# Attention, two networks: k times v with its mixed block last, and the weight work of the last two tiles of the first network held back

## The chip, the cores and the metric

One core of a Trainium2 chip. The time is that of the device for one execution, in microseconds (us). The kernel before has a median of 899.63 us over 3 runs (899.12 to 900.37).

## The reference

```python
def phi(x):                       # x: 4 batches, 8 heads, 576 positions, 64 dims; omega: 128 x 64
    proj = np.einsum('bhsd,md->bhsm', x, omega)
    sq = np.sum(x * x, axis=-1, keepdims=True) / 2.0
    h = proj - sq
    h = h - np.max(h, axis=-1, keepdims=True)
    return np.exp(h) / np.sqrt(m)
q_p, k_p = (phi(q_s), phi(k_s))
kv = np.einsum('bhsm,bhsd->bhmd', k_p, v)
z = np.sum(k_p, axis=2)
num = np.einsum('bhsm,bhmd->bhsd', q_p, kv)
den = np.einsum('bhsm,bhm->bhs', q_p, z)[..., None] + 1e-06
x = num / den                     # then as 2304 tokens of 512
h = x @ w_in                      # 512 x 2048
y = (h * (1.0 / (1.0 + np.exp(-1.702 * h)))) @ w_out
out = ((y @ w_a) * (y @ w_b)) @ w_out2     # 512 x 1536, twice, and 1536 x 512
```

q, k, v, omega and the output are float32, the weights float64. The kernel works in float16 pairs: every number is a high part and a low part (the rest), and a product is three matmuls, high by high, high by low and low by high.

## The kernel before

**Stages.** The attention of batch b gives one tile of 512 tokens (4 blocks of 128 positions a head); the 64 positions left over in each batch are collected to a fifth tile of 256, the rest tile. While the first network works on tile b - 1, the attention of batch b and the preparation of weights run beside it as generators, one step of each a turn (`side_step`, `run`). The last two tiles of the first network, tile 3 (512 tokens) and the rest tile, have no attention beside them. Then the second network runs over all tiles.

**k times v (lines 508 to 534, batches 2 and 3).** For each pair of heads there are nine blocks of k features (`e16`, high and low): four of the first head, four of the second, and a mixed block, index 2 * NT = 8, which holds the left-over rows of both heads and writes 130 columns where the others write 65. All nine sum up in one PSUM bank `pk`. The pool of such banks (`att`) has two, which the projections of all head pairs and `pk` share; a projection's bank comes free when ScalarE has read it (the exponentials, line 446). The mixed block is the last to be converted (lines 456, 457).

**One unit of the first network (lines 648 to 687).** `h_unit(f)` makes 128 hidden features: 12 matmuls into `ph`, tanh on ScalarE (line 662), `th` on VectorE (665), the high part `gh` on ScalarE (671), the low part `gl` on VectorE (672). `y_unit(f)` multiplies gh and gl by w_out, 12 matmuls. The order on TensorE is y(f), h(f+2), y(f+1), h(f+3), and so on; `ph` has two banks. `main` yields after each of them, 32 times in a 512 tile, 30 times in the rest tile.

**Weight work (`w_ops`, lines 203 to 278).** The weights come as 64-bit numbers and are made into float16 pairs in chunks of 1 MB. A chunk is: a load on SP's queue; on VectorE three integer operations of 1024 elements (lines 214, 254, 262); for the second network four sums of 256 elements into a scratch tile `sx` (line 248); high parts on ScalarE (272); low parts on VectorE (221: 512, 256 and 1024 elements). It is cut into five steps, in this order: line 214 of this chunk and 254; low parts of the chunk before; 262; the sums and high parts; 214 of the next chunk. The chunks 20 to 25 (NWE to NW2: 31 steps) belong to the last two tiles. `run` asks for `rate` steps for each yield of the tile; inside `tc.issue_after(ins)` each instruction on the engine of `ins` is queued behind `ins`, instructions of other engines are not.

```python
    def run(gen, rate, wmax):
        due = 0.0
        for _ in gen:
            due += rate
            if rate < 1:
                with tc.issue_after(own["nb"]):
                    w_steps(int(due), wmax)
```

`own["nb"]` is the last bias of an attention phase (line 486). In tile 3 no attention is left, so it is long past.

**The forms (`y_forms`, lines 731 to 767).** For the second network (seven products in place of eight) sums of quarters of y are made, split in high and low parts on ScalarE (745) and VectorE (741). Their scratch tile `ts` has the tag `sx` as the weight sums have, with one buffer. `y_forms(0)` is written in the rest tile, one step a yield; `y_forms(1)` in the second network, whose tiles `sums` open when the first network's memory closes.

**What sets the order.** The kernel is written in one order; the framework then makes each engine's queue from it as a list: of what is ready on an engine, the earliest written goes first, and a later one goes when nothing earlier is ready. The queue is fixed when the program is built, and an engine takes it in order.

Of the kernel before, what the change touches and what calls it, by code (L numbers as in the profile page):

```python
# [33 lines left out]
def fused_kernel(  # L34
# [13 lines left out]
    nc = tc.nc  # L48
    B, H, S, D = q.shape
# [4 lines left out]
    NT = 4  # L54
# [6 lines left out]
    T = 2 * NT + 1  # L61
# [125 lines left out]
    NW2 = len(chunks)  # L187
# [97 lines left out]
    def w_steps(n, upto):  # L285
        for _ in range(n):
            if w_done[0] < upto:
                w_done[0] = next(w_gen)
# [13 lines left out]
    own = {}  # L302
# [34 lines left out]
    def a_load(pool, kind, b, hp, queue=nc.sync):  # L337

        if b >= B or (kind, b, hp) in raws:
            return  # L340
        src = {"q": q, "k": k}[kind]
        h0 = 2 * hp
        place = kind
        if b == 0 and hp == NHP - 1:
            place = {"q": "k", "k": "q"}[kind]
        t = pool.tile([P, T, D], F32, tag=f"raw{place}", name=f"raw{kind}_{b}_{hp}", bufs=RAW[place])
        queue.dma_start(
            out=t[:, 0 : 2 * NT, :].rearrange("p (h t) d -> p h (t d)", h=2),
            in_=src[b, h0 : h0 + 2, 0:SM, :].rearrange("h (p t) d -> p h (t d)", t=NT),
        )  # L350
        queue.dma_start(out=t[:, 2 * NT, :], in_=src[b, h0 : h0 + 2, SM:S, :])
        raws[kind, b, hp] = t
# [149 lines left out]
    def kv_parts(hp, pk, scale):  # L502
        nc.scalar.activation(out=kvh[:, hp], in_=pk, func=AF.Copy, scale=scale)
        nc.vector.scalar_tensor_tensor(
            out=kvl[:, hp], in0=pk, scalar=scale, in1=kvh[:, hp], op0=ALU.mult, op1=ALU.subtract
        )

    def kphase32(pool, b, hp, psp, nxt, f32=True):
        nm = f"k{b}_{hp}"
        a_load(pool, "k", b, hp)  # L510
        raw = raws["k", b, hp]
        vt, vm = own["vt"][:, 2 * hp : 2 * hp + 2], own["vm"][:, hp]
        if not f32:
            e16 = pool.tile([P, 2, T, P], F16, tag="e16", name=f"e16_{nm}")
            yield from features(pool, nm, raw, e16, None, psp, nxt)
            v16 = pool.tile([P, 2, 2, NT + 1, VC], F16, tag="xf", name=f"v16_{nm}")
            for o, i in (v16[:, :, :, 0:NT], vt), (v16[:, :, :, NT], vm):
                nc.scalar.activation(out=o[:, 0], in_=i, func=AF.Copy, scale=S_V)
                nc.vector.scalar_tensor_tensor(
                    out=o[:, 1], in0=i, scalar=S_V, in1=o[:, 0], op0=ALU.mult, op1=ALU.subtract  # L520
                )
            yield
            pk = psp()[:, 0 : 2 * VC].rearrange("p (h c) -> p h c", h=2)
            for t in (2 * NT, *range(2 * NT)):
                hs, u = (slice(0, 2), NT) if t == 2 * NT else (t // NT, t % NT)
                eh, el = e16[:, 0, t], e16[:, 1, t]
                vh, vl = v16[:, 0, hs, u], v16[:, 1, hs, u]
                nc.tensor.matmul(pk[:, hs], eh, vh, start=(t == 2 * NT), stop=False)
                nc.tensor.matmul(pk[:, hs], eh, vl, start=False, stop=False)
                nc.tensor.matmul(pk[:, hs], el, vh, start=False, stop=(t == 2 * NT - 1))  # L530
            yield
            kv_parts(hp, pk, S_KV / (S_E * S_V))
            yield
            return
        e32 = pool.tile([P, T, M], F32, tag="e16", name=f"e32_{nm}")
        yield from features(pool, nm, raw, None, e32, psp, nxt)
        pk = psp()[:, 0 : 2 * VC].rearrange("p (h c) -> p h c", h=2)
        nc.tensor.matmul(pk, e32[:, 2 * NT, :], vm, start=True, stop=False)
        for t in range(2 * NT):
            nc.tensor.matmul(  # L540
                pk[:, t // NT], e32[:, t, :], vt[:, t // NT, t % NT, :], start=False, stop=(t == 2 * NT - 1)
            )
        yield
        nc.scalar.copy(own["kv"][:, hp], pk)
        yield
# [98 lines left out]
    def ffn1(j, xh, xl, n):  # L644

        gh, gl, yacc, phs = {}, {}, {}, {}
# [11 lines left out]
        def h_unit(f, cs=range(KC)):  # L658
            h_products(f, cs)
            ph = phs.pop(f)  # L660
            th = mp.tile([P, 512], F32, tag="f32", name=f"th{j}_{f}")
            nc.scalar.activation(  # L662
                out=th[:, :n], in_=ph[:, :n], func=AF.Tanh, scale=0.5 * 1.702 / (S_X * S_W)
            )
            nc.vector.scalar_tensor_tensor(  # L665
                out=th[:, :n], in0=th[:, :n], scalar=1.0, in1=ph[:, :n], op0=ALU.add, op1=ALU.mult
            )
            GS = 0.5 * S_G / (S_X * S_W)
            a = gp.tile([P, 512], F16, tag="gh", name=f"gh{j}_{f}")
            b = gp.tile([P, 512], F16, tag="gl", name=f"gl{j}_{f}")  # L670
            nc.scalar.activation(out=a[:, :n], in_=th[:, :n], func=AF.Copy, scale=GS)  # L671
            nc.vector.scalar_tensor_tensor(  # L672
                out=b[:, :n], in0=th[:, :n], scalar=GS, in1=a[:, :n],
                op0=ALU.mult, op1=ALU.subtract,
            )
            gh[f], gl[f] = a, b

        def y_unit(f):
# [48 lines left out]
    def y_load(j, n):  # L727
        yfs[j] = late["pool"].tile([P, KC, 512], F32, tag="yf", name=f"yf{j}", bufs=1)
        nc.sync.dma_start(out=yfs[j][:, :, :n], in_=ys[j][:, :, :n])
# [299 lines left out]
    def side_step():  # L1029

        while waiting and waiting[0][0] <= turn[0]:
            live.append(waiting.pop(0)[1])
        for g in list(live):
            if next(g, live) is live:
                live.remove(g)
        turn[0] += 1
# [15 lines left out]
        waiting.append((turn[0] + t, counted(b, gen)))  # L1052
        waiting.sort(key=lambda w: w[0])

    def run(gen, rate, wmax):

        due = 0.0
        for _ in gen:
            due += rate
            if rate < 1:  # L1060
                with tc.issue_after(own["nb"]):
                    w_steps(int(due), wmax)
            else:
                w_steps(int(due), wmax)
            due -= int(due)
            side_step()

    def finish_side(b):
        while left[b]:
            side_step()  # L1070
# [58 lines left out]
    following = []  # L1129
# [14 lines left out]
    def next_tile(b, make):  # L1144
        def made():
            finish_side(b)
            following.append(make())
            return following[-1]

        return made  # L1150
# [49 lines left out]
                    run(head(following[-1], 3), 11 / 32, NW1 + 2)  # L1200
                run(following[-1][0](ahead, 3 if b == 2 else 2), 11 / 32, (NW1 + 2, NWE)[b - 2])
    late["pool"] = ctx.enter_context(tc.tile_pool(name="late", bufs=1))
    run(following[-1][0](next_tile(B - 1, rest_tile)), 18 / 32, NW2)
    y_load(0, SM)
    fg = y_forms(0, SM)
    for i, _ in enumerate(following[-1][0]()):
        next(fg, None)
        if i % 2:
            w_steps(1, NW2)
    for _ in fg:  # L1210
        pass
    w_need(NW2)
# [39 lines left out]
```

## Time and profile before

| | |
|---|---|
| median of 3 runs | 899.63 us (899.12 to 900.37) |
| the profiled execution | 899.4 us, its span 897.6 us |
| TensorE matmul (PE) busy | 872.3 us, 97% |
| VectorE (DVE) busy | 690.9 us, 77% |
| ScalarE (ACT) busy | 455.3 us, 51% |
| tile 3 on TensorE | some 386 to 468 us |
| the rest tile on TensorE | some 468 to 513 us |

Times in the rows are from the span's start. PE is TensorE, DVE VectorE, ACT ScalarE, SP the queue that issues most transfers. The time of a matmul in its row is longer than the distance to the next one's start, since they are pipelined; the same holds in small for VectorE.

### The profile page before, as it was taken

The page shows a single profiled execution, that of the slowest core. Times are in us where ns is not written, and L with a number is a line of the kernel's source. Part 1 is how long each engine was busy: PE and PEld are TensorE (multiplying, and loading weights), DVE is VectorE, ACT ScalarE, POOL GpSimd, SP SyncE. Part 2 cuts the span into 40 slices and gives each one's busy share as a digit, 9 for nine tenths or more (in the row PEclk, how much of TensorE's full clock was granted, in tenths as well). Part 3 has the DMA queues.
Part 4 walks back from the last instruction along what each step waited for, and adds up shares of the span by engine and source line. Part 5 has one row for each costly group of instructions (what it writes and reads, how often), then busy time and mean ns, then how long its engine had stood idle before and what let it go on. Part 6 is the DMA issues. An engine that isn't in the chain of part 4 may idle for free.

```text
span 897.6 us, 17390 instructions
## 1 busy us (share of the span) xinstructions
PE 872.3 (97%) x7094; PEld 626.3 (70%) x7094; DVE 690.9 (77%) x1244; ACT 455.3 (51%) x1087; POOL 1.4 (0%) x10
## 2 busy tenths in 40 slices
PE   8999999999999999999999999999999999999997
PEld 6864555644554455444448888888888888888886
DVE  5889999778797787999923399777999558566766
ACT  7777774677566776454323354544443122233221
POOL 0000000000000000000000000000000000000000
PEclk9999999999999999999999999999999999999999
DMA  7856895453674323885401055212332022223312
GB/s 205 242 142 162 205 228 197 120 120 82 137 161 110 75 40 67 146 259 222 135 7 49 24 177 175 106 43 83 134 126 83 5 40 84 83 99 125 87 39 71
DMA packets 129343, 105.35 MB, mean 117 GB/s; under 512 B 97776, under 2 KB 111088, under 8 KB 127216
## 3 DMA queue, kind: packets, MB, share of 16 engines
q1 hardware_dynamic: 128558, 103.66, 41.2%
q8 instruction: 55, 0.90, 0.4%
q10 hardware_dynamic: 706, 0.59, 0.2%
q14 instruction: 24, 0.20, 0.1%
HBM read 71.07 MB, written 17.69 MB: 99 GB/s over the span
## 4 chain that ended last, share of the span: by engine, by line
PE 59%; DVE 21%; DMA 7%; ACT 7%; issue 2%; ACTq 0%; SPq 0%; DVEq 0%
PE ph L655 3%; PE ph L654 3%; PE ph L656 3%; PE y L685 3%; PE y L686 3%; PE y L687 3%; DMA xt_k<-x_k 3%; PE oA L904 2%; PE oA L902 2%; PE oA L903 2%; PE pbA L811 2%; PE pbA L809 2%; PE pbA L810 2%; PE paA L809 2%; PE pa L568 2%
## 5 line engine op out<-in xcount | busy, mean ns | idle before, releaser
L686 PE MATMUL y<-gl,w_out 128*128 128x512 f16 (+1 forms) x320 | 114.4, 358 | 0.9 <-DVE gl L672 0.8
L687 PE MATMUL y<-gh,w_out 128*128 128x512 f16 (+1 forms) x320 | 114.2, 358 | 0.0
L685 PE MATMUL y<-gh,w_out 128*128 128x512 f16 (+1 forms) x320 | 111.9, 358 | 0.8 <-ACT gh L671 0.7
L654 PE MATMUL ph<-xT,w_in 128*128 128x512 f16 x256 | 97.1, 379 | 1.5 <-DMA xT<-x_q_3x 0.7
L655 PE MATMUL ph<-xT,w_in 128*128 128x512 f16 x256 | 97.1, 379 | 0.3 <-DVE xT L623 0.3
L656 PE MATMUL ph<-xT,w_in 128*128 128x512 f16 x256 | 97.1, 379 | 0.0
L665 DVE SCALAR_TENSOR_TENSOR th<-th,ph 128x512 f32<-128x512 f32 (+1 forms) x80 | 50.3, 629 | 39.9 <-ACT th L662 39.7
L662 ACT ACTIVATE th<-ph 128x512 f32<-128x512 f32 (+1 forms) x80 | 44.2, 553 | 48.8 <-PE ph L656 48.8
L671 ACT ACTIVATE gh<-th 128x512 f16<-128x512 f32 (+1 forms) x80 | 47.1, 588 | 42.0 <-DVE th L665 41.9
L672 DVE SCALAR_TENSOR_TENSOR gl<-th,gh 128x512 f16<-128x512 f32 (+1 forms) x80 | 50.7, 634 | 15.9 <-ACT gh L671 15.5
L809 PE MATMUL paA<-forms,w_a 128*128 128x256 f16 (+1 forms) x240 | 61.0, 262 | 1.6 <-DVE ca L828 0.8
L809 PE MATMUL pbA<-forms,w_b 128*128 128x256 f16 (+1 forms) x240 | 61.1, 262 | 0.9 <-DVE cb L828 0.9
L811 PE MATMUL pbA<-forms,w_b 128*128 128x256 f16 (+1 forms) x240 | 61.0, 262 | 0.0
L811 PE MATMUL paA<-forms,w_a 128*128 128x256 f16 (+1 forms) x240 | 61.0, 262 | 0.0
L810 PE MATMUL pbA<-forms,w_b 128*128 128x256 f16 (+1 forms) x240 | 61.0, 262 | 0.0
L810 PE MATMUL paA<-forms,w_a 128*128 128x256 f16 (+1 forms) x240 | 61.0, 262 | 0.0
L902 PE MATMUL oA<-w_o,ab 128*128 128x256 f16 x216 | 58.9, 273 | 1.6 <-ACT ab L860 0.9
L904 PE MATMUL oA<-w_o,ab 128*128 128x256 f16 x216 | 58.9, 273 | 0.6 <-DVE ab L861 0.5
L903 PE MATMUL oA<-w_o,ab 128*128 128x256 f16 x216 | 58.9, 273 | 0.0
L817 ACT COPY ka<-paA 128x512 f32<-128x512 f32 (+1 forms) x30 | 16.3, 543 | 78.2 <-PE paA L811 78.1
L910 DVE SCALAR_TENSOR_TENSOR o<-oA,o 128x512 f32<-128x512 f32 (+1 forms) x45 | 28.5, 633 | 34.2 <-PE oA L904 34.2
L687 PEld LDWEIGHTS <-w_out 128*128 128x128 f16 x320 | 31.4, 98 | 29.9 <-issue 3.0
(209 smaller groups left out, 2353.5 us busy)
## 6 DMA issues: line engine op xcount, KB each, us to landing
wraw<-in_moe_w_out_dram SPq DMA_DIRECT2D x14, 1024.0 KB
forms<-fd SPq DMA_DIRECT2D x8, 1792.0 KB
wraw<-in_moe_w_in_dram SPq DMA_DIRECT2D x8, 1024.0 KB
fd<-forms SPq DMA_DIRECT2D x4, 1792.0 KB
wraw<-in_moe_w_a_dram SPq DMA_DIRECT2D x6, 1024.0 KB
wraw<-in_moe_w_b_dram SPq DMA_DIRECT2D x6, 1024.0 KB
vt<-in_v_dram SPq DMA_DIRECT2D x16, 256.0 KB
rawq<-in_q_dram SPq DMA_DIRECT2D x16, 256.0 KB
```

The source lines that it names most:

```text
L654: nc.tensor.matmul(ph[:, :n], w[:, 0, c, fs], xh(c), start=(c == 0), stop=False)
L655: nc.tensor.matmul(ph[:, :n], w[:, 0, c, fs], xl(c), start=False, stop=False)
L656: nc.tensor.matmul(ph[:, :n], w[:, 1, c, fs], xh(c), start=False, stop=(c == KC - 1))
L685: nc.tensor.matmul(o, w[:, 0, f % 4, cs], gh[f][:, :n], start=(f == 0), stop=False)
L686: nc.tensor.matmul(o, w[:, 0, f % 4, cs], gl[f][:, :n], start=False, stop=False)
L687: nc.tensor.matmul(o, w[:, 1, f % 4, cs], gh[f][:, :n], start=False, stop=(f == FC1 - 1))
L809: nc.tensor.matmul(o[:, i], wh, xh, start=first, stop=False, skip_group_check=True)
L810: nc.tensor.matmul(o[:, i], wh, xl, start=False, stop=False, skip_group_check=True)
L811: nc.tensor.matmul(o[:, i], wl, xh, start=False, stop=final, skip_group_check=True)
L902: nc.tensor.matmul(bank[:, t], lh, wh, start=first, stop=False, skip_group_check=True)
L903: nc.tensor.matmul(bank[:, t], lh, wl, start=False, stop=False, skip_group_check=True)
L904: nc.tensor.matmul(bank[:, t], ll, wh, start=False, stop=final, skip_group_check=True)
```

## The change

The mixed block goes last in k times v. The weight steps of tile 3 are queued behind `gl` of the newest unit in place of `nb`, at 14 in 32 yields in place of 18; those of the rest tile are queued behind `gl` too, where nothing held them, at two in three yields in place of one in two.

```diff
-            for t in (2 * NT, *range(2 * NT)):
+            for t in range(T):
                 hs, u = (slice(0, 2), NT) if t == 2 * NT else (t // NT, t % NT)
                 eh, el = e16[:, 0, t], e16[:, 1, t]
                 vh, vl = v16[:, 0, hs, u], v16[:, 1, hs, u]
-                nc.tensor.matmul(pk[:, hs], eh, vh, start=(t == 2 * NT), stop=False)
-                nc.tensor.matmul(pk[:, hs], eh, vl, start=False, stop=False)
-                nc.tensor.matmul(pk[:, hs], el, vh, start=False, stop=(t == 2 * NT - 1))
+                nc.tensor.matmul(pk[:, hs], eh, vh, start=(t == 0), stop=False, skip_group_check=True)
+                nc.tensor.matmul(pk[:, hs], eh, vl, start=False, stop=False, skip_group_check=True)
+                nc.tensor.matmul(pk[:, hs], el, vh, start=False, stop=(t == T - 1), skip_group_check=True)
...
-            nc.vector.scalar_tensor_tensor(
+            own["gl"] = nc.vector.scalar_tensor_tensor(
                 out=b[:, :n], in0=th[:, :n], scalar=GS, in1=a[:, :n],
                 op0=ALU.mult, op1=ALU.subtract,
-            )
+            ).ins
...
-    def run(gen, rate, wmax):
+    def run(gen, rate, wmax, behind="nb"):
...
-                with tc.issue_after(own["nb"]):
+                with tc.issue_after(own[behind]):
                     w_steps(int(due), wmax)
...
-    run(following[-1][0](next_tile(B - 1, rest_tile)), 18 / 32, NW2)
+    run(following[-1][0](next_tile(B - 1, rest_tile)), 14 / 32, NW2, "gl")
     y_load(0, SM)
     fg = y_forms(0, SM)
     for i, _ in enumerate(following[-1][0]()):
         next(fg, None)
-        if i % 2:
-            w_steps(1, NW2)
+        if i % 3:
+            with tc.issue_after(own["gl"]):
+                w_steps(1, NW2)
```

## Rows read from the trace of the kernel before

**Rows 1.** Busy time by stage: tile 3, rest tile, start of the second network; clock, DMA.

```profile
core 0: us, PE busy (x) PEld busy (x) DVE busy (x) ACT busy (x) POOL busy (x), PEclk, DMA share, GB/s
...
386.00:468.00 82.00, 81.17 (x373) 36.38 (x372) 64.43 (x100) 35.53 (x59) 0.00 (x0) 1.00 0.46 154
468.00:513.00 45.00, 44.94 (x398) 38.72 (x397) 14.25 (x33) 15.14 (x38) 0.00 (x0) 1.00 0.07 25
513.00:560.00 47.00, 46.39 (x425) 41.25 (x423) 45.06 (x64) 24.64 (x42) 0.00 (x0) 1.00 0.52 177
```

**Rows 2.** Waits of TensorE: us in total, times, longest.

```profile
PE y L686 <- DVE gl L672: 0.8, 2, 0.4
...
PE ph L654 <- DMA xT<-x_q_3x: 0.7, 1, 0.7
```

**Rows 3.** What line 528, first matmul of a block, waited for (us, times).

```profile
  DVE sx L248: 0.8, 1
  ACT e_q L446: 0.6, 3
  ACT e_k L446: 0.4, 1
```

**Rows 4.** Timeline of TensorE: start, length, operation, [idle before].

```profile
205.15 0.22 PE L528 MATMUL pa<-v_k,e_k 128*128 128x130 f16 x1 [0.79 <-DVE sx L248]
```

**Rows 5.** Timeline of VectorE ahead of it: low half of the mixed block.

```profile
203.10 0.28 DVE L457 SCALAR_TENSOR_TENSOR e_k<-e_k,e_k 128x128 f16<-128x128 f32 x1
```

**Rows 6.** Timeline of ScalarE ahead of it: exponentials of another head pair.

```profile
203.97 1.12 ACT L446 ACTIVATE e_k<-pa,nb_k 128x128 f32<-128x128 f32 x4
```

**Rows 7.** Timeline of VectorE, end of tile 2: weight operations among the normalisations.

```profile
372.87 0.66 DVE L214 TENSOR_SCALAR wf<-wraw 128x1024 int32<-128x1024 int32 x1
...
373.91 1.22 DVE L254 SCALAR_TENSOR_TENSOR wf<-wraw,wf 128x1024 int32<-128x1024 int32 x1
...
377.77 1.22 DVE L262 SCALAR_TENSOR_TENSOR wf<-wraw,wf 128x1024 int32<-128x1024 int32 x1
```

**Rows 8.** Timeline of TensorE in tile 3: a wait on gl.

```profile
407.33 0.38 PE L685 MATMUL y<-gh,w_out 128*128 128x512 f16 x1
408.13 0.38 PE L686 MATMUL y<-gl,w_out 128*128 128x512 f16 x1 [0.42 <-DVE gl L672]
```

**Rows 9.** Timeline of VectorE in tile 3: operations back to back.

```profile
420.83 0.69 DVE L214 TENSOR_SCALAR wf<-wraw 128x1024 int32<-128x1024 int32 x1
421.43 0.68 DVE L665 SCALAR_TENSOR_TENSOR th<-th,ph 128x512 f32<-128x512 f32 x1
...
424.77 1.22 DVE L254 SCALAR_TENSOR_TENSOR wf<-wraw,wf 128x1024 int32<-128x1024 int32 x1
425.91 0.42 DVE L248 TENSOR_TENSOR sx<-wf,sx 128x256 f32<-128x256 f32 x1
426.24 0.69 DVE L665 SCALAR_TENSOR_TENSOR th<-th,ph 128x512 f32<-128x512 f32 x1
426.84 1.02 DVE L221 SCALAR_TENSOR_TENSOR w_b<-wf,w_b 128x512 f16<-128x512 f32 x2
```

**Rows 10.** Timeline of VectorE in tile 3: first subtractions of the forms of tiles 0 and 1.

```profile
406.19 0.68 DVE L741 TENSOR_TENSOR ts<-yf 128x512 f32<-128x512 f32 x1
...
439.34 0.69 DVE L741 TENSOR_TENSOR ts<-yf 128x512 f32<-128x512 f32 x1
```

**Rows 11.** Timeline of VectorE in the rest tile: gl of unit 3, unit 4, th of 5 and 15.

```profile
480.46 0.43 DVE L672 SCALAR_TENSOR_TENSOR gl<-th,gh 128x256 f16<-128x256 f32 x1 [0.48 <-ACT gh L671]
...
483.10 0.43 DVE L672 SCALAR_TENSOR_TENSOR gl<-th,gh 128x256 f16<-128x256 f32 x1 [0.48 <-ACT gh L671]
484.75 0.42 DVE L665 SCALAR_TENSOR_TENSOR th<-th,ph 128x256 f32<-128x256 f32 x1 [1.23 <-ACT th L662]
...
510.95 0.42 DVE L665 SCALAR_TENSOR_TENSOR th<-th,ph 128x256 f32<-128x256 f32 x1 [1.29 <-ACT th L662]
```

**Rows 12.** Timeline of TensorE in the rest tile: where gl of 483.10 is used.

```profile
484.25 0.27 PE L686 MATMUL y<-gl,w_out 128*128 128x256 f16 x1
```

**Rows 13.** Timeline of VectorE, first operation after the rest tile.

```profile
514.50 0.69 DVE L741 TENSOR_TENSOR forms<-yf,forms 128x512 f16<-128x512 f32 x1 [2.21 <-ACT forms L745]
```

## The prediction

> **What bounds the kernel now.** I read the windows by stage first. TensorE works 81.17 of 82 us in the fourth batch's tile (386 to 468 us) and 44.94 of 45 in the rest tile (468 to 513), at a granted clock of 1.00, the 2.4 GHz level [rows 1]. So only a removed TensorE wait can bring time, and any new wait costs in full. The same rows show what the change plays with: VectorE is busy 64.43 of 82 us in the first stretch, 14.25 of 45 in the second and 45.06 of 47 at the start of the second network. The 33 operations in the rest tile are little more than its own 32 passes (th and gl of 16 units): the weight work written there has floated forward into tile 3.
>
> Then the waits of TensorE. Two of 0.4 us on gl and one of 0.7 us on the transposed x of the last head pair belong to this weight work [rows 2]; the blocks of k times v have five waits, 1.8 us together [rows 3].
>
> **The change, part by part.**
>
> Order in k times v. Instructions and columns stay the same, 27 matmuls in each of 8 blocks, so nothing is saved in work. The question is what the first matmul waits for. At 205.15 [rows 4] the low half of the mixed block had been done since 203.38 [rows 5], but the ScalarE exponentials that free the PSUM bank ended at 203.97 + 1.12 = 205.09 [rows 6]. The other four waits are put down to exponentials too [rows 3]. Whichever block goes first needs that bank, so I take 0. Bounds: all five waits go (-1.8), or each of the 8 blocks is placed earlier than its bank is free and waits 0.1 us more (+0.8).
>
> Tail of tile 2. Three weight operations of the first held chunk (L214, L254, L262) stand at 372.87, 373.91 and 377.77 among the normalisations that make the last x [rows 7]. In the changed kernel the first step is written behind gl of tile 3's third unit and is held there. The chain loses up to 0.60 + 1.14 + 1.14 us of VectorE time, more than the 0.7 us wait on its transpose [rows 2]. I take the wait as gone. The loads that SP issues for chunks are not held (the hold binds VectorE alone) and have two buffers, so they come earlier than their use in any case: 0.
>
> Tile 3. 18 steps become 14, about one in 2.3 yields, each behind the newest gl. The two gl waits [rows 2] should go: a unit pair of 24 matmuls at 0.215 us is 5.2 us, two VectorE passes of 0.60 and one step of at most 2.07 fill little of it. A wait costs more than its listed idle: from the matmul at 407.33 to the next at 408.13 are 0.80 us instead of 0.215, so 0.58 against the listed 0.42 [rows 8]. With that 0.16 on each of three waits, the gain here and in the tail is 0.8 + 0.7 + 0.5 = **2.0 us**. Bounds: 0.7 (only the wait on x goes) and 2.4.
>
> Rest tile. What left must be done here. Start-to-start times of VectorE are 1.14 us for 1024 elements, 0.60 for 512 (and for L214), 0.33 for 256 [rows 9]. A chunk is therefore 0.60 + 1.14 + 1.14 + 4 x 0.33 (sums) + 0.60 + 0.33 + 1.14 (low parts) = 6.27 us. There are 31 steps for the six chunks 20 to 25; step 14 is the sums of chunk 22 and falls on tile 3's last yield, so 17 steps are left. The forms of tile 0 (y_forms) come along: their scratch tile has the tag of the sums and one buffer, handed on in the order written. In the kernel before they ran at 406.19, just behind chunk 22 [rows 10]. Now that buffer comes free with the low parts of chunk 22, step 17, held behind gl of rest unit 3. That gl starts at 480.46 [rows 11]; the forms cannot start earlier, though nothing holds them.
>
> So, between 480.79 and 510.95, when the last unit's th is due [rows 11], VectorE has to do: low parts of chunk 22 (2.07), the rest of chunk 23 (4.53), chunks 24 and 25 (12.54), the forms on the scratch tile (6 x 0.60 + 1.14 = 4.74) and 22 passes of the units themselves (7.26). That is 31.1 us in 30.2: VectorE becomes the bound of this stage.
>
> The loss is not even. Units 0 to 3 run freely. Then the low parts, the forms and step 18 (1.14) are written ahead of unit 5's th and are ready, so they stand in front of it: with unit 4's two passes 2.07 + 4.74 + 1.14 + 0.66 = 8.6 us, where 484.75 - 480.79 = 4.0 are free. A unit's gl, at 483.10 + 0.43 = 483.53, is used at 484.25 [rows 11, 12], so 0.72 us of lateness is covered and 3.9 would reach TensorE. The forms wait in between for their ScalarE casts, and th of unit 5 can slip into such gaps; I take 3.3. At the end the low parts of chunk 25 (2.07) are held behind gl of unit 14, with 484.75 - 483.10 - 0.33 = 1.3 us until the next th; the last unit has no products between its own and its use, so 0.7 goes to TensorE. Together **4.0 us**. Bounds: 0.5 (the units' passes always come first and the weight work spills over), and 7: the 3.9 in full, 0.7, and 0.2 for each of 12 units for an operation of up to 1.14 us caught in front of th or gl.
>
> How long an operation holds VectorE decides this term. The rows show starts 0.60 us apart for operations recorded as 0.69 [rows 9]. The Trainium skill (VectorE: DVE Perf Modes, The DRAIN you can't avoid) says that the next operation does not start until the pipeline is empty; read as the recorded length, this would add an estimated 0.09 us to each of some 60 operations, 5 us more. The rows speak against this reading.
>
> Start of the second network. Three subtractions of the next forms, at 439.34 and after [rows 10], and the first three operations of each of the next two chunks, which also ran ahead, move to beyond 512: 3 x 0.60 + 2 x 2.88 = 7.6 us. There VectorE idles 2.21 us once [rows 13] and is otherwise full [rows 1], but much of that is weight work needed later. I take 0.3 (0 to 2).
>
> **Sum.** 0 - 2.0 + 4.0 + 0.3 = +2.3 us. The profiled execution took 899.4 us (span 897.6 and 1.8 around it), 0.23 under the median of 899.63. So 901.7 for it, and about **901.8** as a median. About 0.2% (1.8 us) is what a measurement of this kernel can tell from no change; the forecast lies just past it.
>
> **The rivals.**
>
> Faster: the units' th and gl always win VectorE in the rest tile, and what doesn't fit runs after 512 beside the second network, whose own passes again go first. For it: tile 3 took all this work on VectorE, 64 of 82 us [rows 1], and TensorE lost little more than the waits of rows 2. Against it: there a unit pair is 5.2 us long, in the rest tile 2.6, with 0.72 us of cover; and the forms are needed by the second network's first products. The rest tile then costs 0.5, the sum is -2.0 + 0.5 + 0.3 = -1.2, and with half of the k times v waits -2.1: 897.5. It decides if the rest tile's unit pairs keep to 2.6 us, less 0.2 in total. Chance 0.18.
>
> No change: the burst costs 1.5 to 2 instead of 3.3 since ScalarE's casts leave more gaps, or the k times v waits do shrink. Sum about +0.3: 899.9. Chance 0.34. Here also belongs that the holds do nothing, because the scheduler had put the steps there anyway; rows 9 speak against that, since chunk 25's shift at 420.83, a step written in the rest tile, ran in tile 3.
>
> Much slower: the forms of tile 1 take their scratch buffer only behind chunk 25 and reach the second network late, where VectorE is full 45.06 of 47 us [rows 1]; another 3 us there, 904.8. Chance 0.07.
>
> Recorded length as occupancy (the rule above): +5 on the forecast, 906.8. Rows 9 bear it out nowhere: chance 0.01.
>
> **How the numbers follow.** The forecast, slower by 1.8 to 4.5, has 0.40. Slower in all 0.40 + 0.07 + 0.01 = 0.48, same 0.34, faster 0.18. The range takes in the no-change case and most of the faster one: 897.3 at the low end (the faster rival and a little more) and 905.0 at the high end (the forecast with the rest tile at its upper bound, -2.0 + 7.0 + 0.3 = 5.3). Left out are some 0.12 below and 0.06 above. The forecast's own range is 901.4 to 904.
>
> **What would show it.** Right: VectorE's busy time in the rest tile rises from 14 to some 38 us and falls in tile 3 to some 45; the forms' first subtraction stands behind 480; TensorE waits there for th, gl or the ph bank, above all between units 4 and 9; no gl wait in tile 3; the wait on x_q_3x gone. Each of the five k times v waits should stand, within 0.2 us, as it is now. Wrong: a rest tile of 45 us with VectorE as full as I say (cover larger than 0.72), k times v waits gone, or new waits in tile 3.

## The result, and the profile after

The changed kernel has a median of 907.95 us (905.91 to 909.92, 6 runs) against 900.17 of the kernel before beside it (899.12 to 902.16, 6 runs): ratio 1.0077, interval 1.0063 to 1.0091. Slower was forecast, but by 2.3 us and at most to 905.0; by the medians it is 7.8 (by the ratio 6.9). The profiled execution took 909.92 us, its span 908.2.

Windows of the kernel after, the stretches and columns of [rows 1]:

```profile
386.00:468.00 82.00, 81.30 (x377) 36.66 (x375) 35.49 (x52) 26.16 (x43) 0.00 (x0) 1.00 0.18 55
468.00:513.00 45.00, 43.48 (x362) 35.16 (x361) 38.07 (x71) 21.59 (x47) 0.00 (x0) 1.00 0.45 159
513.00:560.00 47.00, 43.68 (x380) 37.67 (x379) 45.24 (x68) 25.79 (x45) 0.00 (x0) 0.96 0.42 142
```

VectorE's busy time went from 64.43 to 35.49 us in tile 3 and from 14.25 to 38.07 in the rest tile; TensorE now has holes in the second and third stretch, and the third shows a mean clock of 0.96. Waits of TensorE after (us in total, times, longest), with the ones that answer to [rows 2, 3]:

```profile
PE paA L809 <- ACT ka L817: 2.9, 2, 2.5
PE y L685 <- ACT gh L671: 1.6, 4, 0.7
PE pa L528 <- DVE sx L248: 0.9, 1, 0.9
PE y L686 <- DVE gl L672: 0.8, 3, 0.4
PE ph L654 <- DVE th L665: 0.7, 2, 0.4
PE pa L528 <- ACT e_q L446: 0.6, 3, 0.2
PE pa L528 <- ACT e_k L446: 0.5, 1, 0.5
```

The wait for x_q_3x is gone; the five waits of k times v stand. New is one of 2.5 us in the second network.

Where the time went is read from the start of the same matmul in both timelines of TensorE (after less before). These shifts are of one execution each: +2.57 at the last k times v, +0.87 at the first h of the rest tile (468.45, now 469.32), +9.66 at its last y (513.10, now 522.76), +10.51 at one third of the second network's products. The first 2.57 are no work of the change (a lower clock between 50 and 100 us, one DMA wait): in the profiles of the runs below, most with the same code up to there, this shift lies between -0.8 and +2.2. So the tail of tile 2 and tile 3 gained 1.7 us, the rest tile lost 8.8, and what follows lost 0.85 more.

Timeline of VectorE in the rest tile after (start, length, operation, idle before): gl of unit 3; the low parts of chunk 22; th; the forms' first subtractions and L262; a later gl; three operations of chunk 26; the last unit's th:

```profile
482.69 0.43 DVE L672 SCALAR_TENSOR_TENSOR gl<-th,gh 128x256 f16<-128x256 f32 x1 [0.48 <-ACT gh L671]
483.03 1.02 DVE L221 SCALAR_TENSOR_TENSOR w_a<-wf,w_a 128x512 f16<-128x512 f32 x2
483.97 1.22 DVE L221 SCALAR_TENSOR_TENSOR w_a<-sx,w_a 128x1024 f16<-128x1024 f32 x1
485.10 0.42 DVE L665 SCALAR_TENSOR_TENSOR th<-th,ph 128x256 f32<-128x256 f32 x1
485.43 0.69 DVE L741 TENSOR_TENSOR ts<-yf 128x512 f32<-128x512 f32 x1
...
486.97 0.69 DVE L741 TENSOR_TENSOR ts<-yf,ts 128x512 f32<-128x512 f32 x1
487.57 1.22 DVE L262 SCALAR_TENSOR_TENSOR wf<-wraw,wf 128x1024 int32<-128x1024 int32 x1
...
505.68 0.42 DVE L672 SCALAR_TENSOR_TENSOR gl<-th,gh 128x256 f16<-128x256 f32 x1 [1.10 <-ACT gh L671]
...
511.93 0.69 DVE L214 TENSOR_SCALAR wf<-wraw 128x1024 int32<-128x1024 int32 x1
...
514.87 1.23 DVE L254 SCALAR_TENSOR_TENSOR wf<-wraw,wf 128x1024 int32<-128x1024 int32 x1
516.13 1.23 DVE L262 SCALAR_TENSOR_TENSOR wf<-wraw,wf 128x1024 int32<-128x1024 int32 x1
...
520.59 0.42 DVE L665 SCALAR_TENSOR_TENSOR th<-th,ph 128x256 f32<-128x256 f32 x1
```

The order is the one foretold: low parts, then the forms on the scratch tile they free [rows 10, 11]. From gl of unit 3 to the last th it takes 37.90 us where it took 30.49.

Ahead of that, the last three of tile 3's 14 steps ran in the rest tile: the low parts of chunk 21 at 469.56, then line 262 and the sums of chunk 22. At tile 3's last yields the newest gl is already that of the rest tile's units 0 and 1, and the steps written there are held behind it:

```profile
472.52 0.43 DVE L672 SCALAR_TENSOR_TENSOR gl<-th,gh 128x256 f16<-128x256 f32 x1 [0.48 <-ACT gh L671]
472.87 1.22 DVE L262 SCALAR_TENSOR_TENSOR wf<-wraw,wf 128x1024 int32<-128x1024 int32 x1
...
476.26 0.43 DVE L672 SCALAR_TENSOR_TENSOR gl<-th,gh 128x256 f16<-128x256 f32 x1 [0.48 <-ACT gh L671]
476.61 0.75 DVE L248 TENSOR_TENSOR sx<-wf 128x256 f32<-128x256 f32 x2
```

TensorE did not stand through all of it. At 489.02 it began with products of the second network, drawn forward into the holes: 40 of their matmuls run before the last y, 4.4 us at 0.109 us from start to start. They were missed after the rest tile. Timeline of TensorE after: the last y, the wait, and matmuls of the same size behind it:

```profile
522.76 0.27 PE L687 MATMUL y<-gh,w_out 128*128 128x256 f16 x1
...
526.43 0.37 PE L809 MATMUL paA<-forms,w_a 128*128 128x256 f16 x1 [2.53 <-ACT ka L817]
...
528.95 0.42 PE L809 MATMUL paC<-forms,w_a 128*128 128x256 f16 x1
...
530.59 0.27 PE L809 MATMUL paA<-forms,w_a 128*128 128x256 f16 x1
```

Timeline of ScalarE after: the copies of y, and the copy that frees the bank waited for:

```profile
522.41 1.22 ACT L699 ACTIVATE ye<-y 128x256 f32<-128x256 f32 x4 [0.95 <-PE y L687]
...
525.78 0.60 ACT L817 COPY ka<-paA 128x512 f32<-128x512 f32 x1
```

The same two in the kernel before:

```profile
512.75 1.21 ACT L699 ACTIVATE ye<-y 128x256 f32<-128x256 f32 x4 [0.93 <-PE y L687]
...
516.12 0.60 ACT L817 COPY ka<-paA 128x512 f32<-128x512 f32 x1
```

The copy comes 3.02 us behind the last y in both. Before, TensorE had 28 matmuls to do meanwhile and waited 0.35 us; now 8 were left, and it waited 2.53. Windows of the kernel after, columns of [rows 1], show what came next:

```profile
526.00:527.00 1.00, 0.57 (x3) 0.41 (x3) 1.00 (x2) 1.00 (x3) 0.00 (x0) 0.60 0.00 0
527.00:529.00 2.00, 2.00 (x12) 1.42 (x10) 2.00 (x4) 1.33 (x2) 0.00 (x0) 0.50 0.00 0
529.00:531.00 2.00, 2.00 (x17) 1.68 (x16) 0.82 (x2) 1.59 (x3) 0.00 (x0) 0.85 0.00 0
```

The clock fell to the 1.2 GHz level. The 12 matmuls from 526.43 to 528.95 took 2.52 us; the 12 from 530.59 took 1.31. With the rest of the slow stretch it cost 1.5 us.

### The profile page after: what moved, and what is told of

Read it like the earlier page. It is cut to its first block, busy times and chain, and to the rows that moved or that the text cites. A ratio compares the mean times of both kernels' runs of the same rounds, so it can differ in the third digit from the quotient of the medians.

```text
span 908.2 us, 17396 instructions
## 1 busy us (share of the span) xinstructions
PE 877.8 (97%) x7094; PEld 628.1 (69%) x7094; DVE 691.1 (76%) x1244; ACT 456.7 (50%) x1087; POOL 1.4 (0%) x10
## 5 line engine op out<-in xcount | busy, mean ns | idle before, releaser
L687 PE MATMUL y<-gh,w_out 128*128 128x512 f16 (+1 forms) x320 | 113.1, 358 | 0.0
L685 PE MATMUL y<-gh,w_out 128*128 128x512 f16 (+1 forms) x320 | 108.7, 357 | 1.6 <-ACT gh L671 1.6
```

The lines of the kernel that those rows point to most:

```text
L685: nc.tensor.matmul(o, w[:, 0, f % 4, cs], gh[f][:, :n], start=(f == 0), stop=False)
L687: nc.tensor.matmul(o, w[:, 1, f % 4, cs], gh[f][:, :n], start=False, stop=(f == FC1 - 1))
```

## The experiments

Medians are beside runs of the kernel before on the same chip. "Rest tile" is the time from its first h to its last y (44.65 us before), read in each run's timeline of TensorE.

**The two halves of the change.** The first run has the order in k times v alone (the first hunk of the diff and nothing else), the second everything but that hunk.

> Only the order in k times v is changed, the weight work is as before. Theory (the blocks wait for their PSUM bank, whichever goes first): 0, within 0.5 us of the kernel before, and the waits in front of line 528 stand. Rival (part of the loss is in this order, as the blocks are placed earlier and wait longer): 1 us or more slower.

> Only the weight work of the last two tiles is held and spread, k times v is as before. Theory (VectorE becomes the bound of the rest tile, and what follows has lost its cover): the whole loss, 7 to 9 us slower than before. Rival (the order in k times v has a share): 1 us or more less than the whole change loses.

The order: 899.6 us against 900.15, ratio 0.9996 (0.9985 to 1.0006). It costs and gains nothing. The rest: 906.62, ratio 1.0083 (1.0067 to 1.0098). By the ratio this is the whole loss. By the medians it is 6.5 us, 1.3 less than the whole change, which the four runs cannot tell apart from it. With the order alone worth nothing, the loss is the weight work. The shift falls from -0.81 at the last k times v to -2.91 at the rest tile (a gain of 2.1), then +8.81 in the rest tile, and the wait on ka is there again, 2.5 us.

**No step in the rest tile.** All steps are asked for in tile 3, at 31 in 32 yields, and held behind gl; k times v is as before (also in the next run). The diffs of both are against the whole change.

```diff
-    run(following[-1][0](next_tile(B - 1, rest_tile)), 14 / 32, NW2, "gl")
+    run(following[-1][0](next_tile(B - 1, rest_tile)), 31 / 32, NW2, "gl")
...
-        if i % 3:
-            with tc.issue_after(own["gl"]):
-                w_steps(1, NW2)
```

> k times v as before; all 31 weight steps are held behind gl in tile 3 (31 of 32 yields), none are left for the rest tile. Theory (the loss is the amount of work moved into the rest tile, the hold itself is good): TensorE gains some 2 us up to the end of tile 3, the rest tile carries only the forms of tile 0 (4.7 us) and costs 0 to 1.5; 0.5 to 2 us faster than before. Rival (the hold itself costs, since a step caught behind gl holds up what follows): tile 3 shows new waits on gl or th, 2 us slower or more.

901.19 against 900.15, ratio 1.0014 (1.0005 to 1.0024): neither the gain that the theory had nor the rival's 2 us. Tile 3 gained 1.5, but the rest tile is still 3.1 longer. What comes last in tile 3's order falls into the rest tile's first units in one lump, VectorE is busy 31.23 us there, and the longest wait of TensorE is:

```profile
474.75 0.27 PE L686 MATMUL y<-gl,w_out 128*128 128x256 f16 x1 [1.18 <-DVE gl L672]
```

**Tile 3 held, the rest tile not.** The steps come at 18 in 32 yields in tile 3, held behind gl, and at one in two, unheld, in the rest tile.

```diff
-    run(following[-1][0](next_tile(B - 1, rest_tile)), 14 / 32, NW2, "gl")
+    run(following[-1][0](next_tile(B - 1, rest_tile)), 18 / 32, NW2, "gl")
...
-        if i % 3:
-            with tc.issue_after(own["gl"]):
-                w_steps(1, NW2)
+        if i % 2:
+            w_steps(1, NW2)
```

> k times v as before; the rates of before (18 in 32, every second yield), tile 3 held behind gl, the steps written in the rest tile not held. Theory (amount): 13 steps in place of 17 are left behind the end of tile 3, 16 us of VectorE work in place of 21; the rest tile is again the place of the loss, about half as large, 2 to 5 us slower than before. Rival (the hold in the rest tile makes the loss): 0 to 2 us faster than before.

901.46 against 900.15, ratio 1.0015 (1.0006 to 1.0024): between the theory's 2 us slower and the rival's gain. The rest tile is 3.1 longer, with VectorE nearly full; window of the rest tile in this run:

```profile
468.00:513.00 45.00, 43.29 (x373) 36.26 (x372) 43.20 (x79) 21.75 (x47) 0.00 (x0) 1.00 0.53 182
```

Between 474 and 511 VectorE has no listed wait at all here. The whole change shows only 38.07 in the same 45 us, but its rest tile goes on for 9.8 us behind them. From the first h to the last y, the whole change and then this run:

```profile
469.32:522.76 53.44, 51.54 (x437) 42.40 (x436) 46.69 (x87) 24.15 (x53) 0.00 (x0) 1.00 0.49 173
```

```profile
467.82:515.56 47.74, 45.87 (x397) 38.58 (x395) 44.24 (x81) 22.52 (x50) 0.00 (x0) 1.00 0.55 187
```

With the hold VectorE has 2.5 us more to do, but the stage is 5.7 longer. That made the hold itself a suspect; the last two runs take it up.

**The forms of tile 0 written ahead of tile 3.** All of the change, but y_load and y_forms(0) are written before tile 3 and take one step a yield there.

```diff
-    run(following[-1][0](next_tile(B - 1, rest_tile)), 14 / 32, NW2, "gl")
     y_load(0, SM)
     fg = y_forms(0, SM)
+
+    def with_forms(gen):
+        for _ in gen:
+            next(fg, None)
+            yield
+
+    run(with_forms(following[-1][0](next_tile(B - 1, rest_tile))), 14 / 32, NW2, "gl")
     for i, _ in enumerate(following[-1][0]()):
-        next(fg, None)
```

> The whole change, but the forms of tile 0 are written at the head of tile 3 in place of the rest tile (their scratch buffer then comes ahead of the weight sums). Theory (amount: the rest tile has 4.7 us too much work on VectorE, and the forms alone are 6.5 us of it): the rest tile loses clearly less, at most 3 us of its stage, and the whole is 1 to 4 us slower than the kernel before in place of 7 to 8. Rival (the weight steps behind gl make the loss by themselves, each catching th or gl of a unit): still 5 us or more slower.

903.25 against 900.24, ratio 1.0038 (1.0026 to 1.0051): the total is the theory's, the stage is not. Taking the forms' 4.7 us of VectorE work out of the rest tile shortens it by 3.1, but it is still 5.7 longer than before, where at most 3 was expected. 13 matmuls run ahead in place of 40, the wait on ka is 0.35 and the clock stays at 1.00.

**Products not drawn forward.** All of the change, and the second network's products are queued behind the rest tile's last matmul.

```diff
-                nc.tensor.matmul(o, w[:, 1, f % 4, cs], gh[f][:, :n], start=False, stop=(f == FC1 - 1))
+                own["y"] = nc.tensor.matmul(
+                    o, w[:, 1, f % 4, cs], gh[f][:, :n], start=False, stop=(f == FC1 - 1)
+                ).ins
...
+            with tc.issue_after(own["y"]):
+                product_now(k, m)
```

> The whole change, and the matmuls of the second network are queued behind the last matmul of the rest tile, so that none of them fills a gap there. Theory (the 2.5 us wait on the copy ka after the rest tile is there because the products that used to cover it had been drawn forward, and the lower clock follows from that wait): the wait is back at some 0.4 us and the clock stays at 1.00, but the gaps in the rest tile, 5.2 us of which these products filled, now stand bare: within 3 us of the whole change, slower rather than faster. Rival (the wait on ka is made by the fuller ScalarE and VectorE queues, whatever TensorE has to do): the wait stays above 2 us and the whole is some 5 us slower than the whole change.

908.2 against 900.24, ratio 1.0087 (1.0073 to 1.0102), as the whole change and as the theory had it. The rest tile is 8.7 longer, now with bare holes (two rows of TensorE's timeline below), but the wait on ka is 0.34 and the clock 1.00. So the products drawn forward bring nothing, and the wait on ka and the clock are not a loss of their own: they are what was saved in the holes and then paid.

```profile
490.40 0.27 PE L654 MATMUL ph<-xTr,w_in 128*128 128x256 f16 x1 [1.74 <-DVE th L665]
...
520.88 0.60 PE L685 MATMUL y<-gh,w_out 128*128 128x256 f16 x4 [1.82 <-ACT gh L671]
```

**All weight work in tile 3, forms first.** Both use the forms as above, k times v as before and no step in the rest tile; the first runs 40 in 32 yields, held, the second 31 in 32, held.

```diff
-            if rate < 1:
-                with tc.issue_after(own["nb"]):
+            if rate < 1 or behind == "gl":
+                with tc.issue_after(own[behind]):
...
+    run(with_forms(following[-1][0](next_tile(B - 1, rest_tile))), 40 / 32, NW2, "gl")
```

```diff
+    run(with_forms(following[-1][0](next_tile(B - 1, rest_tile))), 31 / 32, NW2, "gl")
```

> k times v as before; forms of tile 0 at the head of tile 3, and all 31 weight steps held behind gl in tile 3 at 40 in 32 yields, so that they end some 7 yields before its end. Theory (amount in the rest tile): the rest tile is bare again and costs nothing, tile 3 keeps what the hold gains: 0.5 to 2 us faster than the kernel before. Rival (a hold at this density makes as many waits in tile 3 as it removes): within 0.5 us of the kernel before or slower.

> k times v as before; forms of tile 0 at the head of tile 3, all 31 steps held in tile 3 at 31 in 32 yields. Beside the run that left the forms in the rest tile (3 us lost there), theory (amount): the rest tile keeps only the last steps' few operations at its head and loses under 1 us; 0 to 1.5 us faster than the kernel before. Rival: the loss at the head of the rest tile comes from the last weight steps, not from the forms, and stays at 2 us or more.

40 in 32: 906.09 against 900.24, ratio 1.0059 (1.0047 to 1.0071), a loss where the theory had a gain; the rival, waits in tile 3, has part of it. In the profiled execution (903.86) VectorE is busy 68.38 us of tile 3's 82, with four waits on gl of 0.28 to 0.71 at its end; then comes a wait that no theory had. Timeline of ScalarE:

```profile
479.79 0.38 ACT L662 ACTIVATE th<-ph 128x256 f32<-128x256 f32 x1 [4.89 <-DMA yd<-ye]
```

Timeline of TensorE:

```profile
480.69 0.27 PE L654 MATMUL ph<-xTr,w_in 128*128 128x256 f16 x1 [2.64 <-DVE th L665]
```

The four buffers that tanh takes are also those of tile 3's outputs, and tanh waits for their store. The DMA engines are full just then, busy for 0.95 and 1.06 of 476 to 478 and 478 to 480, against 0.02 and 0.04 in the kernel before, and two weight loads were issued ahead of the stores; that these held the store up is not shown.

31 in 32: 900.63, ratio 1.0005 (0.9993 to 1.0017). The gain up to the rest tile (2.1 in its profile) and a rest tile 2.4 longer cancel; the rival is right, the last steps cost that much without the forms.

**One fixed hold, no hold by unit.** Both start from the kernel before, and the rest tile is as there. In the first the steps of tile 3 are queued behind the last normalisation of the fourth batch, in the second behind the newest gl of the first nine yields and no later one.

```diff
-                with tc.issue_after(own["nb"]):
+                with tc.issue_after(own["nb"] if behind is None else behind):
...
-    run(following[-1][0](next_tile(B - 1, rest_tile)), 18 / 32, NW2)
+    run(following[-1][0](next_tile(B - 1, rest_tile)), 18 / 32, NW2, own["last", B - 1].ins)
```

```diff
-                with tc.issue_after(own["nb"]):
+                if i < behind:
+                    own["held"] = own["gl"]
+                with tc.issue_after(own["held" if behind else "nb"]):
...
-    run(following[-1][0](next_tile(B - 1, rest_tile)), 18 / 32, NW2)
+    run(following[-1][0](next_tile(B - 1, rest_tile)), 18 / 32, NW2, 9)
```

> The kernel before (its order in k times v, rates and unheld rest tile), with one fixed hold: the weight steps of tile 3 are queued behind the last normalisation of the fourth batch (line 629) in place of nb, and float freely after it. Theory (the loss is the VectorE work that is left for the rest tile; the gain at the tail is separate from it): the 0.7 us wait for x_q_3x goes, tile 3 has room for the three operations, VectorE's busy time in 468 to 513 stays at 14 to 17 us, the rest tile stays 44.8 to 45.3 long: 0.4 to 1.0 us faster, ratio 0.9989 to 0.9996. Rival (a late start of the weight work is not made up in tile 3 and comes out in the rest tile, or new gh and gl waits at tile 3's start take the gain back): within 0.3 of the kernel before.

> As the run before this one, but the fixed hold is later: the steps of tile 3's first nine yields are queued behind the newest gl, all later ones only behind the gl of the ninth yield; rest tile unheld, 18 in 32 yields. It moves some 10 us of VectorE work out of the tail and the first units. Theory (amount of work in the rest tile against its cover): what tile 3 cannot make up, some 5 to 10 us, stands in the rest tile, VectorE there busy 19 to 27 us of 45, and being unheld it gives way to nobody: first gaps of 0.3 to 1.5 in the rest tile; together 0.5 faster to 0.7 slower. Rival (only the hold by unit, not the amount, costs): rest tile as before, 0.4 to 1.0 us faster.

Both 1.0001 (0.9992 to 1.0010): 899.74 and 900.34 against 899.95. In the first the wait for x_q_3x and the two on gl of [rows 2] go and four others come, one of 0.54 at 445.60 and three at tile 3's start; its rival is right. Timeline of TensorE:

```profile
391.00 0.38 PE L686 MATMUL y<-gl,w_out 128*128 128x512 f16 x1 [0.38 <-DVE gl L672]
...
397.41 0.59 PE L685 MATMUL y<-gh,w_out 128*128 128x512 f16 x2 [1.29 <-ACT gh L671]
398.49 0.38 PE L686 MATMUL y<-gl,w_out 128*128 128x512 f16 x1 [0.48 <-DVE gl L672]
```

In the second, VectorE's busy time in the rest tile is 20.50 us and the rest tile is 1.8 longer, 1.0 of that in holes for gh and gl at 478, as its theory had it: even 6 us more cost, when they fall on the first units.

**ScalarE's casts held as well.** On the first of these two, the casts of the forms of tile 0 are queued behind gh of an early unit; then that alone, on the kernel before.

```diff
+            if behind is not None and i == 5:
+                own["cast"] = own["gh"]
...
-            nc.scalar.copy(s[:, 0], x)
+            if j:
+                nc.scalar.copy(s[:, 0], x)
+            else:
+                with tc.issue_after(own["cast"]):
+                    nc.scalar.copy(s[:, 0], x)
```

> The fixed hold behind the last normalisation, and the ScalarE casts of the forms of tile 0 queued behind the high part gh of tile 3's early units instead of ahead of tanh at some 386. In the run with the hold alone the cast stood in ScalarE's queue at 386.08, waited 1.63 us for the load of yf and took 1.57, and TensorE waited 0.38, 1.29, 0.48 and 0.54 us for gh and gl at 391.0, 397.4, 398.5 and 445.6. Theory (the gain at the tail was given back by that cast, which kept ScalarE from tanh and from the copies of y): the waits at 391 to 399 go, some 2.4 us, the wait at 445.6 stays: 1.5 to 2.7 faster than before, ratio 0.9970 to 0.9984, and the fastest of all. Rival (the late weight work itself keeps VectorE from th and gl there): the waits stay, within 0.5 of the kernel before.

> The kernel before with only the casts of the forms of tile 0 queued behind gh of an early unit of tile 3; weight work as before. Theory: the cast cost nothing here (at 391.36 it waited only 0.19 for its load, behind other work), so the same within 0.5 us; the 0.7 us wait for x_q_3x and the two waits on gl stay. Rival (the cast holds ScalarE up in the kernel before as well): 0.5 to 1.2 faster.

0.9993 (0.9979 to 1.0006) and 1.0006 (0.9991 to 1.0022): no difference that these runs can tell. The first interval still touches the smallest gain of its theory (0.9984). But in the profiles the time from the last k times v to the rest tile is 0.39 us longer than before with the casts held and without, so they were hardly what took the gain back. With them out of the way waits still stand, in other places; TensorE's timeline of the first:

```profile
394.24 0.38 PE L685 MATMUL y<-gh,w_out 128*128 128x512 f16 x1 [0.70 <-ACT ye L699]
398.46 0.38 PE L686 MATMUL y<-gl,w_out 128*128 128x512 f16 x1 [0.61 <-DVE gl L672]
```

**Hold against amount.** The whole change without the hold in the rest tile; and the kernel before with that hold alone.

```diff
         if i % 3:
-            with tc.issue_after(own["gl"]):
-                w_steps(1, NW2)
+            w_steps(1, NW2)
```

```diff
         if i % 2:
-            w_steps(1, NW2)
+            with tc.issue_after(own["gl"]):
+                w_steps(1, NW2)
```

> The whole change with one line undone: the weight steps of the rest tile (two in three yields, as in the change) are no longer queued behind gl. The amount of VectorE work left for the rest tile is the same, 17 steps and the forms. Theory H (the hold in the rest tile, not the amount of work, makes the loss larger than forecast: while the newest gl waits for ScalarE's gh, nothing held behind it can run, and VectorE, which is the bound there, stands idle): VectorE runs with hardly a wait between 475 and 512, no products are drawn forward, from the first h of the rest tile to the last y some 48 us in place of 53.4 (44.65 before), the wait on ka 0.35, the clock 1.00: 902 to 903.5, ratio 1.002 to 1.004. Rival A (the amount of VectorE work makes the loss): the rest tile stays at 52 to 53.5 and the total at 906 to 908.

> The kernel before with one line added: the weight steps of its rest tile (one in two yields) are queued behind the newest gl; tile 3 as before, so 13 steps are left and the forms of tile 0 run in tile 3. Theory H: the held steps now stand in the rest tile, with VectorE waits for gh and th between them; VectorE has some 14 + 17 us of work in 45 there and is not the bound, so the loss is lateness of single gl and th against a cover of 0.72 us: rest tile 0.5 to 2.5 longer, 900.5 to 902.5, ratio 1.0005 to 1.003. Rival A (by amount alone, 31 us in 45 fits): within 0.5 of the kernel before. Above 903 neither holds.

Without the hold: 904.05 against 900.42, ratio 1.0042 (1.0028 to 1.0055), just above what theory H had (902 to 903.5) and well below rival A's 906. The rest tile is 51.1 us long, 6.5 longer in place of 8.8, where H had 48 and A 52 or more: neither theory is right alone. The hold is 2.3 of the 8.8. In the total it is 4.1 us by the medians and 3.2 by the ratios, about half of the loss, since the clock now stays at 1.00 and the wait on ka is shorter, 1.8 us. (It is not 0.35, though only 14 matmuls ran ahead: ScalarE does a further cast of the forms before the copy, which comes 5.14 us behind the last y.) VectorE does not wait once between 480 and 512; just ahead of that it waits once, 1.10 us at 479.17, for a weight load. Windows of this run:

```profile
480.00:490.00 10.00, 8.63 (x74) 6.95 (x72) 9.98 (x19) 4.67 (x10) 0.00 (x0) 1.00 0.21 56
490.00:500.00 10.00, 9.60 (x86) 8.21 (x85) 10.00 (x20) 5.28 (x11) 0.00 (x0) 1.00 0.94 366
500.00:510.00 10.00, 9.95 (x89) 8.43 (x87) 10.00 (x20) 4.51 (x10) 0.00 (x0) 1.00 0.30 107
```

The hold alone: 903.12 against 900.42, ratio 1.0028 (1.0018 to 1.0037), the rest tile 2.8 longer although VectorE is busy only 29.99 us of 45. That is a little past the upper ends of theory H (902.5 and 2.5), and above 903 neither was to hold. Rival A's no change is out. But this run moves work as well as holding it: VectorE's busy time in tile 3 falls from 64.43 to 42.27 us, since held steps cannot run ahead, so its 2.8 us are not the price of the hold alone. What a hold does is seen in VectorE's timeline of this run: th comes late, behind held work; gl then waits for ScalarE's gh, and the next weight operation, a step held behind that gl, waits with it:

```profile
494.00 0.41 DVE L665 SCALAR_TENSOR_TENSOR th<-th,ph 128x256 f32<-128x256 f32 x1
495.50 0.42 DVE L672 SCALAR_TENSOR_TENSOR gl<-th,gh 128x256 f16<-128x256 f32 x1 [1.10 <-ACT gh L671]
495.85 0.68 DVE L214 TENSOR_SCALAR wf<-wraw 128x1024 int32<-128x1024 int32 x1
```

Side by side, against 44.65 us of rest tile before. The first column is the window from 468 to 513 (14.25 us before), which ends before a long rest tile does; the second runs from each run's own first h to its last y (13.87 us before).

| run | VectorE busy, 468 to 513, us | VectorE busy, own rest tile, us | rest tile longer by, us |
|---|---|---|---|
| whole change | 38.07 | 46.69 | 8.8 |
| products behind | 38.44 | 46.67 | 8.7 |
| rest tile unheld | 43.85 | 49.13 | 6.5 |
| forms first | 36.86 | 42.24 | 5.7 |
| only tile 3 held | 43.20 | 44.24 | 3.1 |
| no step in the rest tile | 31.23 | 32.13 | 3.1 |
| only the rest tile held | 29.99 | 33.11 | 2.8 |
| 31 in 32, forms first | 25.83 | 27.57 | 2.4 |
| hold to the ninth yield | 20.50 | 20.29 | 1.8 |

Two things act. One is the amount. Where VectorE is nearly full without a hold (the third and fifth line), its work sets the length: the run with only tile 3 held had done 4.1 us more in tile 3 (41.53 against 37.41) and is 3.4 shorter here. The other is the hold. Undone alone, it gives back 2.3 us, though VectorE then has 2.4 us more to do in the stage; and forms first, which is held, has 2.0 us less to do than only tile 3 held and is 2.6 longer. No run changes the hold and leaves the amount exactly the same. In the last four lines VectorE is not full: there the moved work stands in front of single units.

No version beats the kernel before by more than its interval; the lowest ratio among those that touch the weight work is 0.9993.

## Why the prediction was wrong in size

**k times v: right.** 0 was forecast; alone it is 0.9996, and the waits stand within 0.1 us of [rows 3].

**Tail and tile 3: right.** 2.0 was forecast, 1.7 came in the change and 2.1 without its first hunk. (These are single profiles: with the order alone, where nothing is changed here, the same stretch is 0.8 longer.) "No gl wait in tile 3" was wrong: two of 0.35 us, for gh and gl, appear at its start, the next thing late when the wait for x had gone. Held at the normalisation alone, such waits take the whole gain back.

**Rest tile: right in mechanism, 4.0 where 8.8 were lost.** It is here that the prediction failed. VectorE is the bound, as it said, but the lateness was priced as one burst and an end against a cover of 0.72 us. Here the bound engine set the length of its stage by all its work and all its own waits. In rows of the kernel after:
- "Units 0 to 3 run freely": 1.4 us were lost by gl of unit 3 (13.37 us behind the first h in place of 12.01). The last three steps of tile 3 ran among these units. The forecast had them in tile 3, because they are written there; what counts is the gl behind which they are held.
- From there to the last th it is 7.4 longer. Of these 0.9 are the forecast's own 31.1 us in 30.2. 2.9 are the three operations of chunk 26 (511.93, 514.87, 516.13: 0.60 + 1.14 + 1.14), which the forecast put beyond 512; written later, they were ready and ran in front of the last units. This is read from the timeline; no run held them back. 2.8 are VectorE's listed waits for gh and th (five, from 0.29 to 1.10). 0.8 are left, unplaced.
- That the hold makes VectorE wait was no term of the sum; undone alone it gives back 2.3 us of the rest tile.

Tile 3's busy time fell to 35.49 us where some 45 was forecast, which the forecast's own terms do not give: 14 steps are 16.7 us and 31 passes of 0.60 are 18.6, together 35.3. That 35.3 is so near is partly luck, since 4.5 us of these steps ran in the rest tile and a pass counts as 0.69 in the busy time.

**Start of the second network: 0.3 forecast, 0.85 more by the shifts, 1.2 with the products behind.** But the 4.4 us drawn forward should have come back after the last y, and did not: 2.2 (2.53 against 0.35) went to the wait on ka, 1.5 to the clock, 1.5 to short waits between 541 and 583. These 5.2 are the 4.4 and the 0.85. The forecast did not see that a hole filled with later work also uses up what covered a later wait.

**The rivals.** Faster and no change fall by the rest tile. Much slower gave 904.8, from the forms of tile 1; they do begin late, at 520.92, but no wait of TensorE after 491 names the forms. The recorded-length rival gave 906.8, near the result, and is not its cause: VectorE's starts at 486.97 and 487.57 are 0.60 us apart behind a recorded 0.69, as in [rows 9].

## What to carry to other kernels

When work is moved into a short stage, add up the receiving engine's whole queue for it: the stage's own passes, the moved work, what is written later and is ready, and the waits that its order forces. Where that came near the stage's length here, the stage grew to that sum, whatever cover a single unit had. When steps are held behind a result, place them by that result's time, not by where they are written. Holding filler work behind the newest result on its engine also stops it from filling the wait ahead of that result; and holes that later products fill are no gain where those products covered the next wait.

## What the runs showed of the hardware

After the wait of 2.53 us, which followed a stage with many short holes, matmuls of 256 columns started 0.21 us apart in place of 0.11, for some 3 us, at a granted clock of 0.50. In the run without the first hunk the same fall comes 1 us behind the same wait. After waits of 1.74 to 1.82 us (products behind; rest tile unheld) the granted clock stayed at 1.00, and so it did after one of 2.64 us (40 in 32), which followed 4 us without a hole: the length of the wait alone did not decide. The Trainium skill (TensorE: Matmul & The Clock Gate, Part 1: The HAM clock gate) says that the clock has two states, 1.2 and 2.4 GHz. The two distances agree, and 0.60 and 0.85 in the windows are then means over both.
